# Attention and gated feed-forward in one kernel: the gain moves from the weights to the rows, the sinks get their own maximum and exp, and the reordering of q and k gets a fixed place

## The chip, the cores and the metric

One core of a Trainium2 chip runs the whole program. The metric is the device time in microseconds of one execution, lower is better. Times of several executions are given as a median with the lowest and highest. A profile is one execution recorded by the hardware profiler. The engines are PE (matmuls; PEld is its weight load), DVE (vector), ACT (activations), POOL (GpSimd) and SP, which here only issues stores. Each engine works through a queue of its own in order.

## The reference

Sliding-window attention with four sink positions for 4 batches, 8 heads, 768 positions and head size 64, followed by an RMS norm and a gated feed-forward layer over the 3072 tokens with 512 channels and 1536 hidden units.

```python
scores = scale * np.matmul(q, k.transpose(0, 1, 3, 2))
keep = is_sink | in_window          # pos < 4, or 0 <= i - j < 128
scores = np.where(keep, scores, -1e9)
a = np.exp(scores - np.max(scores, axis=-1, keepdims=True))
a = a / (np.sum(a, axis=-1, keepdims=True) + 1e-09)
x = np.matmul(a, v)                 # heads side by side: 3072 x 512
xn = x / np.sqrt(np.mean(x * x, axis=-1, keepdims=True) + 1e-06) * rms_g
g = xn @ w_gate
out = (g * (1.0 / (1.0 + np.exp(-g))) * (xn @ w_val)) @ w_out
```

## The kernel before

**Units.** The attention is cut into 48 half tiles, numbered n: a tile of 128 positions of one batch (24 tiles, six to a batch), and in it half 0 (heads 0 to 3) or half 1 (heads 4 to 7). `a_unit(n)` multiplies q and k of four heads into PSUM, for 128 keys of the tile before and 128 of its own (L269; L264 in the first tile of a batch, which has only its own keys). DVE then folds the older half into the newer with a mask (L281; L275 in the first tile), because each pair of query and column has exactly one of the two inside the window. The four sink scores, computed once a batch by `sink_unit`, are copied in front of the 128 folded scores (L285), the maximum over 132 columns is taken (L288), and ACT takes four exps (L293). POOL copies the four sink probabilities of each head into a small tile PK (L299). `b_unit` transposes the four heads and PK on PE (L308, L312), ACT copies the result out (L317), and POOL splits it with two triangular selections into the newer part cur (L325) and the older part old (L329). `c_unit` multiplies by v (L341, L348, L353), divides by the sum (L362, L363), and after half 1 takes the sum of squares (L370), of which POOL makes the reciprocal root rr (L372, L376). `d_unit` scales the row by rr (L384), transposes it (L389) and copies it into XNT (L392).

**Feed-forward.** Eight groups of three tiles. `f_unit` makes one of twelve blocks of hidden units: gate matmuls pg and value matmuls pl (L407), tanh on ACT (L412), two multiplications on DVE (L414, L418). The sigmoid is written with tanh, so the value weights carry a factor of one half. `o_unit` multiplies by the output weights (L424), ACT copies (L429), SP stores.

**The gain.** `fold_w` multiplies both weight matrices by the RMS gain, in quarters, four row blocks each: 32 instructions on DVE (L133, L137) in all.

**q and k.** `load_qk` brings half a batch with GpSimd transfers (L97), `order_unit` reorders it on DVE (q scaled, L190; k copied, L194), `qk_unit` transposes it on PE (L204) and copies it to QT (ACT, L210) and KT (DVE L214 for the lower, ACT L218 for the upper partitions), two heads at a time. `sink_unit` ends with a copy (L237) and, for the first 128 queries with sinks, a mask on POOL (L240).

**Order.** The prologue issues on POOL, in this order: q and k of batch 0 (four transfers), v of three tiles, then the weights in quarters (two transfers each, L126) with v of the other three tiles behind the first quarter, and wo (L174). Then batch 0 is reordered, transposed and its sinks made, half by half. After that there are slots, one for each n: slot n holds `a_unit(n)`, `c_unit(n-2)`, `b_unit(n-1)` and, for even n, `d_unit`. The work for batch b is put into slots relative to its first one (base = 12 b): loads of q and k at base-11, of v at base-10 to base-5, reordering at base-7 and base-5, transposes at base-6 to base-3, sinks at base-2 and base-1. The first nine slots run alone; from the tenth on six slots at a time are woven with the blocks of one feed-forward group. The program's text is only a priority: a planner places each instruction into its engine's queue when its own model says that the inputs are there, so that an instruction of a later slot can stand ahead of one of an earlier slot.

Of the kernel before, what the change touches and what calls it, by code (L numbers as in the profile page):

```python
# [16 lines left out]
P = 128  # L17
# [4 lines left out]
def kernel(  # L22
# [64 lines left out]
    PK = [const.tile([P, P], BF16, name=f"PK{i}") for i in range(3)]  # L87
# [32 lines left out]
    rmsg = const.tile([P, KTN], FP32, name="rmsg")  # L120
    nc.sync.dma_start(out=rmsg, in_=moe_rms_g.rearrange("(kt p) -> p kt", p=P))
# [8 lines left out]
    def fold_w(c):  # L130
        cols = slice(c * CW, (c + 1) * CW)
        for kt in range(KTN):
            nc.vector.tensor_scalar(  # L133
                out=wg_bf[:, kt, cols], in0=wg_bf[:, kt, cols],
                scalar1=rmsg[:, kt:kt + 1], scalar2=None, op0=ALU.mult,
            )
            nc.vector.tensor_scalar(  # L137
                out=wv_bf[:, kt, cols], in0=wv_bf[:, kt, cols],
                scalar1=rmsg[:, kt:kt + 1], scalar2=0.5, op0=ALU.mult, op1=ALU.mult,
            )  # L140

# [5 lines left out]
    for i in range(3):  # L147
        nc.gpsimd.memset(PK[i], 0.0)
# [25 lines left out]
    nc.gpsimd.dma_start(out=wo_bf, in_=moe_w_out.rearrange("(ft p) d -> p ft d", p=P))  # L174
# [3 lines left out]
    PS = {}  # L178
# [5 lines left out]
    def order_unit(b, half):  # L184

        for nm in ("q", "k"):
            so = stage.tile([P, NT, 4, D], BF16, name=f"{nm}so", tag="so", bufs=4)
            src = ST.pop((nm, b, half)).rearrange("p h (j d) -> p j h d", j=NT)
            if nm == "q":
                nc.vector.tensor_scalar(  # L190
                    out=so, in0=src, scalar1=scale, scalar2=None, op0=ALU.mult,
                )
            else:
                nc.vector.tensor_copy(out=so, in_=src)  # L194
            SO[(nm, b, half)] = so
# [27 lines left out]
    def sink_unit(b, half):  # L223

        par = b % 2
        ps = psum.tile([P, 512], FP32, name="psk", tag="b1")
        for t in range(1, NT):
            for hi in range(2):
                hp = 2 * half + hi
                c0 = (t * 2 + hi) * 2 * NS  # L230
                nc.tensor.matmul(
                    out=ps[:, c0:c0 + 2 * NS].rearrange("p (h s) -> p h s", s=NS),
                    lhsT=QT[par][:, hp, t * P:(t + 1) * P], rhs=KT[par][:, hp, :, 0:NS],
                    start=True, stop=True,
                )
        sk = spool.tile([P, NT, 4, NS], FP32, name="sk", tag="sk", bufs=4)
        nc.vector.tensor_copy(  # L237
            out=sk[:, 1:NT], in_=ps[:, 4 * NS:NT * 4 * NS].rearrange("p (t h s) -> p t h s", s=NS, h=4),
        )
        nc.gpsimd.affine_select(  # L240
            out=sk[:, 1], in_=sk[:, 1], compare_op=ALU.is_ge, fill=NEG,
            base=0, pattern=[[0, 4], [-1, NS]], channel_multiplier=1,
        )
        SINK[(b, half)] = sk
# [9 lines left out]
    def a_unit(n):  # L254
# [19 lines left out]
        if t == 0:  # L274
            nc.vector.copy_predicated(  # L275
                out=sc[:, :, P:2 * P], mask=m_first.unsqueeze(1).to_broadcast((P, 4, P)),
                data=negbig.unsqueeze(2).to_broadcast((P, 4, P)),
            )
            c0 = P
# [8 lines left out]
        nc.vector.tensor_reduce(  # L288
            out=nmax, in_=sc[:, :, c0:2 * P], axis=AX.X, op=ALU.max, negate=True,
        )  # L290
        ps = spool.tile([P, 4, NS + P], BF16, name="ps", tag="ps", bufs=3)
        for h in range(4):
            nc.scalar.activation(  # L293
                out=ps[:, h, c0 - W0:], in_=sc[:, h, c0:2 * P], func=ACT.Exp,
                bias=nmax[:, h:h + 1], scale=1.0,
            )
        PS[n] = ps
        if t > 0:
            nc.gpsimd.tensor_copy(  # L299
                out=PK[n % 3].rearrange("p (h c) -> p h c", c=32)[:, :, 0:NS], in_=ps[:, :, 0:NS],  # L300
            )

    def b_unit(n):
        t = (n // 2) % NT
        ps = PS.pop(n)
        pp = psum.tile([P, 512], FP32, name="pp", tag="b1").bitcast(BF16)
        for h in range(4):
            nc.tensor.transpose(  # L308
                out=pp[:, h * P:(h + 1) * P], in_=ps[:, h, NS:NS + P], identity=ident,
            )  # L310
        if t > 0:
            nc.tensor.transpose(  # L312
                out=pp[:, 4 * P:5 * P], in_=PK[n % 3], identity=ident,
            )
        w = 5 * P if t > 0 else 4 * P
        pt = ppool.tile([P, 5 * P], BF16, name="pt", tag="pt")
        nc.scalar.copy(out=pt[:, 0:w], in_=pp[:, 0:w])  # L317
        if t == 0:
# [5 lines left out]
        pv4 = pt[:, 0:4 * P].rearrange("p (h c) -> p h c", h=4)  # L324
        nc.gpsimd.affine_select(  # L325
            out=cur, in_=pv4, compare_op=ALU.is_ge, fill=0.0,
# [3 lines left out]
            out=old, in_=pv4, compare_op=ALU.is_gt, fill=0.0,  # L330
            base=0, pattern=[[0, 4], [-1, P]], channel_multiplier=1,
        )
        PT[n] = (pt, cur.rearrange("p h c -> p (h c)"), old.rearrange("p h c -> p (h c)"))

    def c_unit(n):
# [4 lines left out]
        if t > 0:  # L340
            nc.tensor.matmul(  # L341
                out=pv[:, 0:4 * VW], lhsT=pt[:, 4 * P:5 * P], rhs=VS[b % 2][:, half, :],
                start=True, stop=False, skip_group_check=True,
            )
        for hh in range(4):
# [33 lines left out]
    def d_unit(bt):  # L379
        g, tb = divmod(bt, GROUP)  # L380
        if tb == 0:
            XNT[g] = xtpool.tile([P, KTN, GN], BF16, name="xnt", tag="xnt")
        xr = xpool.tile([P, DM], BF16, name="xr", tag="xr")
        nc.vector.tensor_scalar(  # L384
            out=xr, in0=X16.pop(bt), scalar1=RR.pop(bt)[:, 0:1], scalar2=None, op0=ALU.mult,
# [35 lines left out]
    def o_unit(g, tb):  # L421
# [7 lines left out]
        nc.scalar.copy(out=osb, in_=po[:, 0:DM])  # L429
# [103 lines left out]
```

## Time and profile before

| | us |
|---|---|
| median of 3 runs (lowest, highest) | 342.35 (342.06, 342.65) |
| profiled execution, its own time | 341.6 |
| its span, first to last instruction | 339.9 |
| busy: PE | 278.8 (82%) |
| busy: DVE | 237.1 (70%) |
| busy: ACT | 193.9 (57%) |
| busy: POOL | 127.8 (38%) |
| scaling of the weights, L133 and L137, 32 instructions | 5.4 + 5.2 |
| copy of the sink scores, L285, 40 instructions | 6.9 |
| copy into PK, L299, 40 instructions | 8.1 |
| mean granted clock of PE | 0.925 |

Busy time is the time in which an engine had at least one instruction running; the chain of waits is followed back from the last instruction to what released it at each step. A time line has the start, the duration, the engine, the line, the operation, out and in, and in brackets the idle time before it and what ended it.

### The profile page before, as it was taken

To read this page: it belongs to the slowest core of one execution; us is meant where nothing else is said; L and a number is where in the kernel's file an instruction comes from. 1 tells how busy PE (TensorE), PEld (TensorE's weight loads), DVE (VectorE), ACT (ScalarE), POOL (GpSimd) and SP (SyncE) were. 2 spreads that over 40 slices of the span, in tenths; PEclk is the share of its full clock that TensorE was granted. 3 is DMA by queue.
4 is the path that set the end of the run, shared out by engine and by line. 5 is a ranking of instruction groups with operands and counts; after the bars stand their busy time and mean duration, and the time that the engine had idled before them with its cause. 6 is when DMAs were issued, how large, how long until landed. Compare 5 with 4: busy or idle time off the path is not lost.

```text
span 339.9 us, 5990 instructions
## 1 busy us (share of the span) xinstructions
PE 278.8 (82%) x2129; PEld 166.3 (49%) x2144; DVE 237.1 (70%) x550; ACT 193.9 (57%) x465; POOL 127.8 (38%) x257
## 2 busy tenths in 40 slices
PE   0451257598998889999988999999889999998994
PEld 0430024365654556556645556655446545554651
DVE  7687274678865897589857883898569837872850
ACT  1371145777566677776666677766566666554321
POOL 8972268889421331322413313214021423122000
PEclk9955555789999999999999999999999999999999
DMA  7999999999801000200010001000100010001002
GB/s 106 188 189 204 206 176 64 172 136 183 54 31 64 0 3 2 92 0 4 23 71 1 2 0 64 31 3 3 62 31 2 0 64 32 3 22 72 0 2 93
DMA packets 43197, 20.83 MB, mean 61 GB/s; under 512 B 26272, under 2 KB 40096, under 8 KB 43168
## 3 DMA queue, kind: packets, MB, share of 16 engines
q0 software_dynamic: 39184, 14.16, 36.5%
q1 hardware_dynamic: 3984, 6.30, 4.9%
q8 instruction: 17, 0.28, 0.3%
q14 instruction: 12, 0.10, 0.1%
HBM read 28.31 MB, written 6.29 MB: 102 GB/s over the span
## 4 chain that ended last, share of the span: by engine, by line
PE 40%; ACT 16%; DVE 14%; POOL 14%; issue 8%; DMA 8%; ACTq 0%; POOLq 0%; DVEq 0%
PE po L424 12%; PE pg L407 10%; PE pl L407 9%; ACT ps L293 7%; DMA qst<-in_q_dram 5%; DVE hT L418 4%; POOL v L106 3%; DVE p L414 3%; DVE nmax L288 3%; DMA v<-in_v_dram 2%; ACT pt L317 2%; PE s L269 2%; ACT th L412 2%; POOL rr L376 2%; POOL cur L325 2%
## 5 line engine op out<-in xcount | busy, mean ns | idle before, releaser
L407 PE MATMUL pg<-xnt,wg_bf 128*128 128x384 bf16 x384 | 79.1, 326 | 4.6 <-DVE hT L418 2.7
L407 PE MATMUL pl<-xnt,wv_bf 128*128 128x384 bf16 x384 | 78.0, 326 | 2.4 <-DVE p L414 1.2
L412 ACT ACTIVATE th<-pg 128x384 bf16<-128x384 f32 x96 | 47.6, 498 | 47.8 <-PE pg L407 46.0
L293 ACT ACTIVATE ps<-s,nmax 128x132 bf16<-128x132 f32 (+1 forms) x192 | 55.5, 372 | 33.9 <-DVE nmax L288 28.8
L424 PE MATMUL po<-wo_bf,hT 128*128 128x512 bf16 x273 | 65.1, 379 | 1.7 <-DVE hT L418 0.9
L414 DVE SCALAR_TENSOR_TENSOR p<-th,pg 128x384 bf16<-128x384 bf16 x96 | 52.5, 548 | 16.5 <-ACT th L412 15.5
L418 DVE TENSOR_TENSOR hT<-p,pl 128x384 bf16<-128x384 bf16 x96 | 52.6, 549 | 3.1
L407 PEld LDWEIGHTS <-wv_bf 128*128 128x128 bf16 x384 | 37.5, 98 | 29.6 <-issue 5.1
L407 PEld LDWEIGHTS <-wg_bf 128*128 128x128 bf16 x384 | 35.3, 98 | 25.5 <-issue 7.4
L299 POOL COPY PK<-ps 128x16 bf16<-128x16 bf16 x40 | 8.1, 203 | 97.7 <-ACT ps L293 97.6
L424 PEld LDWEIGHTS <-hT 128*128 128x128 bf16 x288 | 27.2, 98 | 30.6 <-DVE hT L418 0.9
L325 POOL TENSOR_SCALAR_AFFINE_SELECT cur<-pt 128x512 bf16<-128x512 bf16 x40 | 26.0, 651 | 41.2 <-ACT pt L317 40.2
L317 ACT COPY pt<-pp 128x640 bf16<-128x640 bf16 (+1 forms) x48 | 33.0, 687 | 12.7 <-PE pp L312 9.5
L281 DVE COPY_PREDICATED s<-m_old,s 128x512 f32<-128x512 int16 x40 | 27.7, 691 | 17.8 <-PE s L269 17.6
L308 PE MATMUL pp<-ident,ps 128*128 128x128 bf16 x192 | 24.7, 232 | 16.7 <-ACT ps L293 16.5
L288 DVE TENSOR_REDUCE nmax<-s 128x4 f32<-128x528 f32 (+1 forms) x48 | 33.5, 698 | 0.5
L269 PE MATMUL s<-KT,QT 128*128 128x512 bf16 x80 | 27.6, 420 | 4.5 <-ACT ps L293 4.5
L308 PEld LDWEIGHTS <-ps 128*128 128x128 bf16 x192 | 15.6, 102 | 26.1 <-ACT ps L293 19.0
L329 POOL TENSOR_SCALAR_AFFINE_SELECT old<-pt 128x512 bf16<-128x512 bf16 x40 | 26.9, 674 | 0.0
L384 DVE TENSOR_SCALAR xr<-x,rr 128x512 bf16<-128x512 bf16 x24 | 10.4, 432 | 20.1 <-POOL rr L376 20.1
L429 ACT COPY osb<-po 128x512 f32<-128x512 f32 x24 | 14.2, 590 | 18.0 <-PE po L424 18.0
L106 POOL DMA_DIRECT2D v<-in_v_dram x24 | 21.4, 903 | 0.9 <-issue 0.7
(64 smaller groups left out, 365.4 us busy)
## 6 DMA issues: line engine op xcount, KB each, us to landing
out_dram<-osb SPq DMA_DIRECT2D x24, 256.0 KB, 2.0
qst<-in_q_dram POOLq DMA_DIRECT2D x8, 384.0 KB, 6.5
kst<-in_k_dram POOLq DMA_DIRECT2D x8, 384.0 KB, 7.0
v<-in_v_dram POOLq DMA_DIRECT2D x24, 128.0 KB, 5.8
wg_bf<-in_moe_w_gate_dram POOLq DMA_DIRECT2D x4, 384.0 KB, 9.7
wv_bf<-in_moe_w_val_dram POOLq DMA_DIRECT2D x4, 384.0 KB, 10.9
wo_bf<-in_moe_w_out_dram POOLq DMA_DIRECT2D x1, 1536.0 KB, 19.6
rmsg<-in_moe_rms_g_dram SPq DMA_DIRECT2D x1, 2.0 KB, 2.2
```

What stands on the lines that cost most here:

```text
L106: nc.gpsimd.dma_start(out=v16[:, :, 0:D], in_=v[b, :, t * P:(t + 1) * P, :].rearrange("h t d -> t h d"),)
L269: nc.tensor.matmul(out=dst, lhsT=lhsT, rhs=KT[par][:, hp, :, (t - 1) * P:(t + 1) * P], start=True, stop=True,)
L288: nc.vector.tensor_reduce(out=nmax, in_=sc[:, :, c0:2 * P], axis=AX.X, op=ALU.max, negate=True,)
L293: nc.scalar.activation(out=ps[:, h, c0 - W0:], in_=sc[:, h, c0:2 * P], func=ACT.Exp, bias=nmax[:, h:h + 1], scale=1.0,)
L308: nc.tensor.transpose(out=pp[:, h * P:(h + 1) * P], in_=ps[:, h, NS:NS + P], identity=ident,)
L317: nc.scalar.copy(out=pt[:, 0:w], in_=pp[:, 0:w])
L325: nc.gpsimd.affine_select(out=cur, in_=pv4, compare_op=ALU.is_ge, fill=0.0, base=0, pattern=[[0, 4], [1, P]], channel_multiplier=-1,)
L407: nc.tensor.matmul(out=dst[:, 0:GN], lhsT=w[:, kt, ft * P:(ft + 1) * P], rhs=xnt[:, kt, :], start=(kt == 0), stop=(kt == KTN - 1),)
L412: nc.scalar.activation(out=th, in_=pg[:, 0:GN], func=ACT.Tanh, scale=0.5)
L414: nc.vector.scalar_tensor_tensor(out=p1, in0=th, scalar=1.0, in1=pg[:, 0:GN], op0=ALU.add, op1=ALU.mult,)
L418: nc.vector.tensor_tensor(out=h_t, in0=p1, in1=pl[:, 0:GN], op=ALU.mult)
L424: nc.tensor.matmul(out=po[:, 0:DM], lhsT=HT[(g, ft)][:, tb * P:(tb + 1) * P], rhs=wo_bf[:, ft, :], start=(ft == 0), stop=(ft == FTN - 1),)
```

## The change

**The gain.** `fold_w` is gone, and the weights stay as loaded. The gain is loaded once as a row that is repeated on all 128 partitions (grow, 32 bits). `d_unit` multiplies the row of x by rr and by grow in one DVE instruction with two tensor inputs. The factor one half moves to the last copy on ACT.

**The softmax.** `sink_unit` also takes the negated maximum of the sink scores for each query and head (sm), on DVE, behind the mask on POOL. `a_unit` no longer copies the sink scores into PSUM: it takes the maximum over 128 columns, then the smaller of the two negated maxima (DVE, 128 x 4), POOL adds it to the sink scores (sd, 128 x 16), and ACT takes four exps of 128 columns and a fifth, of the 16 sink values, which it writes straight into the place to be transposed. One tile PS of five blocks takes the place of ps and PK; the POOL copy L299 is gone.

**The reordering.** Each of the two DVE instructions of `order_unit` is pinned by `keep_in_program_order`, which ties an instruction to the one traced just before it on its engine: it can't be queued ahead of that one. The loads of q and k of batch 1 move into the prologue, ahead of wo; those of the later batches go to base-11 and base-10. The reordering goes to base-4 and base-3, the transposes of both head pairs of a half to base-3 and base-2, the sinks to base-2 and base-1.

```diff
+    grow = const.tile([P, DM], FP32, name="grow")
+    nc.sync.dma_start(
+        out=grow, in_=moe_rms_g.rearrange("(o d) -> o d", o=1).to_broadcast((P, DM)),
+    )
...
+    load_qk(1, 0)
+    load_qk(1, 1)
     nc.gpsimd.dma_start(out=wo_bf, in_=moe_w_out.rearrange("(ft p) d -> p ft d", p=P))
...
-                nc.vector.tensor_copy(out=so, in_=src)
+                ins = nc.vector.tensor_copy(out=so, in_=src)
+
+            tc.keep_in_program_order(ins)
...
-        SINK[(b, half)] = sk
+        sm = spool.tile([P, NT, 4], FP32, name="sm", tag="sm", bufs=4)
+        nc.vector.tensor_reduce(
+            out=sm[:, 1:NT], in_=sk[:, 1:NT], axis=AX.X, op=ALU.max, negate=True,
+        )
+        SINK[(b, half)] = (sk, sm)
...
-            nc.vector.tensor_copy(out=sc[:, :, W0:P], in_=SINK[(b, half)][:, t])
-            c0 = W0
         nmax = small.tile([P, 4], FP32, name="nmax", tag="nmax")
         nc.vector.tensor_reduce(
-            out=nmax, in_=sc[:, :, c0:2 * P], axis=AX.X, op=ALU.max, negate=True,
-        )
-        ps = spool.tile([P, 4, NS + P], BF16, name="ps", tag="ps", bufs=3)
+            out=nmax, in_=sc[:, :, P:2 * P], axis=AX.X, op=ALU.max, negate=True,
+        )
+        ps = PS[n % 3]
+        if t > 0:
+            sk, sm = SINK[(b, half)]
+            nc.vector.tensor_tensor(out=nmax, in0=nmax, in1=sm[:, t], op=ALU.min)
+            sd = small.tile([P, 4, NS], FP32, name="sd", tag="sd")
+            nc.gpsimd.tensor_tensor(
+                out=sd, in0=sk[:, t], in1=nmax.unsqueeze(2).to_broadcast((P, 4, NS)), op=ALU.add,
+            )
         for h in range(4):
             nc.scalar.activation(
-                out=ps[:, h, c0 - W0:], in_=sc[:, h, c0:2 * P], func=ACT.Exp,
-                bias=nmax[:, h:h + 1], scale=1.0,
-            )
-        PS[n] = ps
+                out=ps[:, h, :], in_=sc[:, h, P:2 * P], func=ACT.Exp, bias=nmax[:, h:h + 1], scale=1.0,
+            )
         if t > 0:
-            nc.gpsimd.tensor_copy(
-                out=PK[n % 3].rearrange("p (h c) -> p h c", c=32)[:, :, 0:NS], in_=ps[:, :, 0:NS],
+            nc.scalar.activation(
+                out=ps[:, 4, :].rearrange("p (h c) -> p h c", c=32)[:, :, 0:NS], in_=sd, func=ACT.Exp,
             )
...
-        nc.vector.tensor_scalar(
-            out=xr, in0=X16.pop(bt), scalar1=RR.pop(bt)[:, 0:1], scalar2=None, op0=ALU.mult,
+        nc.vector.scalar_tensor_tensor(
+            out=xr, in0=X16.pop(bt), scalar=RR.pop(bt)[:, 0:1], in1=grow, op0=ALU.mult, op1=ALU.mult,
         )
...
-        if g == 0 and ft % FPC == 0:
-            fold_w(ft // FPC)
...
-        nc.scalar.copy(out=osb, in_=po[:, 0:DM])
+        nc.scalar.activation(out=osb, in_=po[:, 0:DM], func=ACT.Copy, scale=0.5)
...
-        for half in range(2):
-            slots[base - 11].append((0.0, lambda b=b, half=half: load_qk(b, half)))
+        if b > 1:
+            for half in range(2):
+                slots[base - 11 + half].append((0.0, lambda b=b, half=half: load_qk(b, half)))
         for half in range(2):
-            slots[base - 7 + 2 * half].append((0.0, lambda b=b, half=half: order_unit(b, half)))
-        for hp in range(HP):
-            slots[base - 6 + hp].append((0.7, lambda b=b, hp=hp: qk_unit(b, hp)))
-        slots[base - 2].append((0.3, lambda b=b: sink_unit(b, 0)))
-        slots[base - 1].append((0.3, lambda b=b: sink_unit(b, 1)))
+            slots[base - 4 + half].append((0.0, lambda b=b, half=half: order_unit(b, half)))
+            for hp in (2 * half, 2 * half + 1):
+                slots[base - 3 + half].append((0.7, lambda b=b, hp=hp: qk_unit(b, hp)))
+            slots[base - 2 + half].append((0.3, lambda b=b, half=half: sink_unit(b, half)))
```

More of the change, by code (lines that the diff above doesn't have):

```diff
@@ L86 @@
     KT = [const.tile([P, HP, 2, S], BF16, name=f"KT{i}") for i in range(2)]
-    PK = [const.tile([P, P], BF16, name=f"PK{i}") for i in range(3)]
+    PS = [const.tile([P, 5, P], BF16, name=f"PS{i}") for i in range(3)]
     VS = [const.tile([P, 2, 4 * VW], BF16, name=f"VS{i}") for i in range(2)]
@@ L119 @@
     wo_bf = const.tile([P, FTN, DM], BF16, name="wo_bf")
-    rmsg = const.tile([P, KTN], FP32, name="rmsg")
-    nc.sync.dma_start(out=rmsg, in_=moe_rms_g.rearrange("(kt p) -> p kt", p=P))
+    grow = const.tile([P, DM], FP32, name="grow")
+    nc.sync.dma_start(
+        out=grow, in_=moe_rms_g.rearrange("(o d) -> o d", o=1).to_broadcast((P, DM)),
+    )
     def load_w(c):
@@ L128, in load_w @@
             )
-    def fold_w(c):
-        cols = slice(c * CW, (c + 1) * CW)
-        for kt in range(KTN):
-            nc.vector.tensor_scalar(
-                out=wg_bf[:, kt, cols], in0=wg_bf[:, kt, cols],
-                scalar1=rmsg[:, kt:kt + 1], scalar2=None, op0=ALU.mult,
-            )
-            nc.vector.tensor_scalar(
-                out=wv_bf[:, kt, cols], in0=wv_bf[:, kt, cols],
-                scalar1=rmsg[:, kt:kt + 1], scalar2=0.5, op0=ALU.mult, op1=ALU.mult,
-            )
     for i in range(2):
@@ L147 @@
     for i in range(3):
-        nc.gpsimd.memset(PK[i], 0.0)
+        nc.gpsimd.memset(PS[i][:, 4, :], 0.0)
     negbig = const.tile([P, 1], FP32, name="negbig")
@@ L177 @@
     PT = {}
-    PS = {}
     PV = {}
@@ L189, in order_unit @@
             if nm == "q":
-                nc.vector.tensor_scalar(
+                ins = nc.vector.tensor_scalar(
                     out=so, in0=src, scalar1=scale, scalar2=None, op0=ALU.mult,
@@ L278, in a_unit @@
             )
-            c0 = P
         else:
@@ L304, in b_unit @@
         t = (n // 2) % NT
-        ps = PS.pop(n)
+        w = 5 if t > 0 else 4
         pp = psum.tile([P, 512], FP32, name="pp", tag="b1").bitcast(BF16)
-        for h in range(4):
+        for h in range(w):
             nc.tensor.transpose(
-                out=pp[:, h * P:(h + 1) * P], in_=ps[:, h, NS:NS + P], identity=ident,
+                out=pp[:, h * P:(h + 1) * P], in_=PS[n % 3][:, h, :], identity=ident,
             )
[L311 to L317, printed above, removed]
+        pt = ppool.tile([P, 5, P], BF16, name="pt", tag="pt")
+        nc.scalar.copy(out=pt[:, 0:w, :].rearrange("p h c -> p (h c)"), in_=pp[:, 0:w * P])
         if t == 0:
@@ L323, in b_unit @@
         old = ppool.tile([P, 4, P], BF16, name="old", tag="old")
-        pv4 = pt[:, 0:4 * P].rearrange("p (h c) -> p h c", h=4)
         nc.gpsimd.affine_select(
-            out=cur, in_=pv4, compare_op=ALU.is_ge, fill=0.0,
+            out=cur, in_=pt[:, 0:4, :], compare_op=ALU.is_ge, fill=0.0,
             base=0, pattern=[[0, 4], [1, P]], channel_multiplier=-1,
@@ L329, in b_unit @@
         nc.gpsimd.affine_select(
-            out=old, in_=pv4, compare_op=ALU.is_gt, fill=0.0,
+            out=old, in_=pt[:, 0:4, :], compare_op=ALU.is_gt, fill=0.0,
             base=0, pattern=[[0, 4], [-1, P]], channel_multiplier=1,
         )
-        PT[n] = (pt, cur.rearrange("p h c -> p (h c)"), old.rearrange("p h c -> p (h c)"))
+        PT[n] = (pt, cur, old)
     def c_unit(n):
@@ L341, in c_unit @@
             nc.tensor.matmul(
-                out=pv[:, 0:4 * VW], lhsT=pt[:, 4 * P:5 * P], rhs=VS[b % 2][:, half, :],
+                out=pv[:, 0:4 * VW], lhsT=pt[:, 4, :], rhs=VS[b % 2][:, half, :],
                 start=True, stop=False, skip_group_check=True,
@@ L348, in c_unit @@
             nc.tensor.matmul(
-                out=dst, lhsT=cur[:, hh * P:(hh + 1) * P], rhs=V16[(b, t)][:, h, :],
+                out=dst, lhsT=cur[:, hh, :], rhs=V16[(b, t)][:, h, :],
                 start=(t == 0), stop=(t == 0), skip_group_check=True,
@@ L353, in c_unit @@
                 nc.tensor.matmul(
-                    out=dst, lhsT=old[:, hh * P:(hh + 1) * P], rhs=V16[(b, t - 1)][:, h, :],
+                    out=dst, lhsT=old[:, hh, :], rhs=V16[(b, t - 1)][:, h, :],
                     start=False, stop=True, skip_group_check=True,
@@ L383, in d_unit @@
         xr = xpool.tile([P, DM], BF16, name="xr", tag="xr")
-        nc.vector.tensor_scalar(
-            out=xr, in0=X16.pop(bt), scalar1=RR.pop(bt)[:, 0:1], scalar2=None, op0=ALU.mult,
+        nc.vector.scalar_tensor_tensor(
+            out=xr, in0=X16.pop(bt), scalar=RR.pop(bt)[:, 0:1], in1=grow, op0=ALU.mult, op1=ALU.mult,
         )
```

## The prediction

> **What bounds the kernel now.** I read the slices of the page first, then the windows, then the time lines of the queues in the first 80 us.
>
> ```profile
> PE   0451257598998889999988999999889999998994
> PEclk9955555789999999999999999999999999999999
> DMA  7999999999801000200010001000100010001002
> 78.00:304.00 226.00, 211.38 (x1667) 126.20 (x1680) 171.06 (x388) 146.93 (x367) 70.45 (x157) 1.00 0.14 30
> 70.69 1.07 PE L407 MATMUL pg<-xnt,wg_bf 128*128 128x384 bf16 x4
> ```
>
> A slice is 8.5 us. There are two stages. From 78 us on the tensor engine is full: 211.4 of 226 us in the window line (its order is PE, PEld, DVE, ACT, POOL), against 171.1 of DVE and 146.9 of ACT. Before that it is mostly idle at a granted clock near 0.5, while the transfers run at nine tenths and more. The border is the first feed-forward matmul at 70.69 us (T0 below); 269 of the 339.9 us follow it. So two questions decide: when does T0 come, and what is added behind it?
>
> What holds T0 is in the two queues that work in order, POOL and DVE:
>
> ```profile
> 18.09 0.22 DVE L237 COPY sk<-psk 128x80 f32<-128x80 f32 x1
> 20.20 0.74 POOL L126 DMA_DIRECT2D wv_bf<-in_moe_w_val_dram  x1 [0.31 <-DMA v<-in_v_dram]
> 21.27 1.87 POOL L174 DMA_DIRECT2D wo_bf<-in_moe_w_out_dram  x1 [0.34 <-DMA v<-in_v_dram]
> 23.15 0.41 POOL L240 TENSOR_SCALAR_AFFINE_SELECT sk<-sk 128x16 f32<-128x16 f32 x2
> 27.56 0.74 POOL L97 DMA_DIRECT2D kst<-in_k_dram  x1 [0.53 <-DMA wg_bf<-in_moe_w_gate_dram]
> 33.25 0.32 DVE L137 TENSOR_SCALAR wv_bf<-wv_bf,rmsg 128x384 bf16<-128x384 bf16 x1 [1.62 <-DMA wv_bf<-in_moe_w_val_dram]
> 35.07 0.71 DVE L288 TENSOR_REDUCE nmax<-s 128x4 f32<-128x528 f32 x1
> 42.79 0.56 DVE L190 TENSOR_SCALAR qso<-qst 128x1536 bf16<-128x1536 bf16 x1 [3.98 <-DMA qst<-in_q_dram]
> ```
>
> To see here: the scaling of the weights stands in DVE's queue ahead of the attention and waits for weights until 33.25 us, so the maximum of half tile n=2 starts only at 35.07; the reordering of batch 1 then waits until 42.79 for its transfer and n=3 is late again. Also: the sink scores of half 0 were copied at 18.09, but their mask (L240) ran on POOL at 23.15, behind all the transfers issued before it in the program. And a transfer's issue waits for an older one. The 17th, 18th, 19th and 23rd issue waited for the landing of the 9th, 10th, 11th and 15th: eight are outstanding, and the ninth blocks POOL. The maxima (L288) start at 19.9, 23.6, 35.1, 43.5, 49.6, 53.6, 60.2, 65.8 and 72.0 us for n=0 to 8.
>
> **What is taken away.** The 32 scalings (10.6 us of DVE) and their waits go, and so do the two stalls just shown. Were that all, n=2 would follow n=1 in about 4.1 us (the quickest step, 49.55 to 53.61) and T0 would come some 12 us sooner (11.5 and 8.4 us for n=2 and n=3 become 4.1 each).
>
> **What replaces it in the head.** The reordering is now kept behind the DVE instruction traced just before it. For half 1 of batch 0 that is the new sink maximum of half 0, which needs L240, which stands on POOL behind every transfer of the prologue, and these now include the four loads of batch 1 ahead of wo. Step by step:
> - wo is now the 23rd transfer; it waits for the 15th, which landed at 27.3 (16.30 plus 11.0). Issue 27.6 to 29.4 (1.87), L240 to 29.7.
> - Sink maximum 0.24 (priced as L237, also 80 elements), two reorderings at 0.56 (median of L190), transposes of k 0.85, two KT copies at 0.95 (L214), the upper copy 0.79 (L218): 34.6. Then for n=1 matmul 0.4, mask 0.75, maximum 0.69, exps 1.15, and for n=2 matmul 1.0 and mask 0.69: the maximum of n=2 starts near 39.8, against 35.07. The weights no longer wait for DVE, but DVE now waits for POOL.
> - POOL's queue is filled with transfers of later slots wherever the planner saw it free: all 26 loads that slots 2 to 31 issue stand between n=2 and n=10, two to five to a slot, and four loads of slot 1 between VS and n=2. From L240 to n=2's new addition (sd) there are now some 11 us with 1.3 us of other POOL work, so I take 8 or more loads there at 0.75 to 0.9 each. The eighth of these is the 31st transfer and waits for the 23rd, wo. wo lands after the 18th (33.2), four loads of q and k at 1.95 (they landed at 42.8, 44.7, 46.7, 48.6) and its own 7.7 (33.2 to 40.9): 48.7. So sd of n=2 comes near 50, and with it the exp behind it on ACT; queued behind that on ACT are the exps of n=3, on them PE's matmul of n=4.
> - From 50: 0.2, exps 1.15, matmul 1.0, mask 0.69, steps between: maximum of n=4 at 53.3 (was 49.6). From there no q/k work is left in the head: 4.1 to 4.7 a step, I take 4.4, so n=7 at 66.5. Before, T0 came 4.9 us after n=7, with 0.96 of q/k transposes ahead of it; now 4.0: T0 at 70.5.
>
> Head: 0.0 us. Its ends: 7 loads or fewer ahead of sd leave n=2 at 39.8, T0 = 39.8 + 5 x 4.4 + 4.0 = 65.8, -4.9; eleven loads, at one landing (1.0) each, +3. The grown load of g (a row for each partition, 256 KB on SP, where 2 KB took 2.2 us) can hold the first q by about 1 us; DVE is at its memsets until 7.8 anyway, and half 1 waits later still, so nothing.
>
> **What moves behind T0.** Of the four q/k units of batch 1 three ran before T0; all four now stand in slots 9 and 10. Each is 12 transposes, 0.67 us on the chain of waits: 3 x 0.67 = +2.0 us on a full PE. Their copies (DVE 0.95, ACT 1.6 a unit) find room: DVE is busy 28.1 of the 36.7 us of that group. Later batches only shift theirs inside the full stage: 0.
>
> **What is added to each tile behind T0** (33 of 40 tiles that have sinks).
>
> ```profile
> L384 DVE TENSOR_SCALAR xr<-x,rr 128x512 bf16<-128x512 bf16 x20 | 8.6, 431 | 18.4 <-POOL rr L376 18.4
> L293 ACT ACTIVATE ps<-s,nmax 128x132 bf16<-128x132 f32 x131 | 38.0, 373 | 14.5 <-DVE nmax L288 11.1 <-PE pv L348 2.0 <-POOL old L329 1.4
> L370 ACT ACTIVATION_READ_ACCUMULATOR sq<-x 128x1 f32 x19 | 4.1, 215 | 0.0
> L363 DVE TENSOR_TENSOR x<-pv,rden 128x256 bf16<-128x256 f32 x38 | 15.9, 418 | 0.2
> ```
>
> - ACT: one exp of 16 elements. No row has it; below, the step of the four exps less their elements (0.26 - 0.10 = 0.16), above, a whole exp (0.37). I take 0.21, the short ACT row: 33 x 0.21 = 6.9 us.
> - DVE: xr gets a second input of 32 bits. From 256 elements (418) to 384 (548) the two-input rows grow by 1.02 ns an element, so 512 take 0.68, against 0.35 undisturbed (median): 20 x 0.33 = +6.6. Six sink maxima +1.4. The minimum takes the place of the copy L285 (0.17; between 0.06, a memset of one column, and 0.18, L362): 0. The shorter maximum -0.4. Sum +7.6.
> - POOL: addition for copy, 0.2 for 0.2, but ACT waits for it. It has the four exps (1.15) as cover: cur and old together are 1.3, so a small part shows only where they stand right ahead.
> - PE: the same transposes; osb and masks as before: 0.
>
> How much reaches the end? In 78 to 304 the chain of waits has 20 of the 45 us of exps (45%) and some 40 of DVE's 171 (23%; hT 5.7, p 4.9, nmax 3.7 and the mask 2.6% of the window, with smaller ones): 3.1 + 1.7. PE's own queue, 94% full, is a second branch that hides part of any delay; I take half, +2.5, between -1 (the POOL copy behind the exps no longer delays the last transpose) and +5.
>
> By the Trainium skill ("ScalarE: Activation LUTs", What ACT_TABLE_LOAD costs) an ACTIVATE with immediate scale and bias takes 186 ns plus 0.833 an element, and neighbours overlap by 93 ns: an estimate of 0.11 for this exp, with which the last sum would be some 0.8 us less; the Trainium skill's 280 plus 0.833 for a pointer bias gives 387 for 128 elements and the trace has 369, so it fits. The Trainium skill ("GPSIMD Engine Reference", Key points) also says that GpSimd shares its SBUF interfaces with VectorE for instructions with two SBUF inputs, which the new xr has; the old xr already ranges from 336 to 819 ns here, so the trace agrees that this operation is stretched, and no run yet shows whether the new form is more so.
>
> **Sum:** 341.6 (the profiled execution's own time: span 339.9 and 1.7 around it) + 0.0 + 2.0 + 2.5 = 346.1. The median of the runs is 0.75 above that execution, so 346.5 for the median, rounded.
>
> **Rivals.**
> 1. *POOL is not blocked* (fewer than eight loads ahead of sd). For it: the count rests on how the planner spreads loads, not on a row. Then the head gives 4.9: 341.6 - 4.9 + 4.5 = 341.2, on the median's scale 342, about no change.
> 2. *The kept place doesn't bind*, half 1 of batch 0 is reordered near 10.6 us as before. Then n=2 waits only for L240 (29.5): T0 between 55.5 (29.5 + 22 + 4.0) and 65 (blocked by wo at n=4 or 5); middle -10, so 336.8. Against it: the program has the maximum ahead of the reordering, and L240 demonstrably stood behind the loads. This is the faster side.
> 3. *Worse:* ACT's new dependence on POOL and DVE's on L240 also cost in the full stage. POOL stands up to 3.5 us waiting for ACT's pt there; it decides from the point where sd or L240 is queued behind such a wait. Six sink maxima at 1 us and eleven loads in the head: 346.5 + 3 + 3 = 352.
>
> **Chances.** Forecast 0.45, rival 1 0.22, rival 2 0.17, rival 3 0.16. This measurement tells about 0.2% (0.7 us) from no change. Faster: 0.16 of rival 2, half of rival 1, 0.06 of the forecast's low end: 0.33. Same 0.09. Slower 0.58. The forecast's own range is 343 to 350; cases of both signs count, so the range goes from within rival 2 to rival 3: 333 to 353.
>
> **What would show it.** L240 behind wo near 29.5; the reordering of half 1 right behind the sink maximum; a load on POOL that waits for wo until about 49, with sd of n=2 behind it; T0 near 70.5; the short exp near 0.2; xr near 0.68. The prediction is wrong if half 1 is reordered before 20 us, if T0 is before 66, or if PE in the full stage stays at its 93.5%.

## The result and the profile after

The changed kernel takes 360.6 us (median of 4 runs, 360.21 to 361.25) against 342.5 for the kernel before (4 runs, 342.06 to 342.68): 1.053 times as long, 95% interval 1.0512 to 1.0553. The forecast was 346.5, with a range up to 353. The direction was right, the size was not. The profiled execution took 361.25 us, with a span of 359.4.

T0, the first feed-forward matmul, is again the border. Slices of the page of the changed kernel (9.0 us each), the time line of PE at T0, and a window of the full stage (length; then busy us of PE, PEld, DVE, ACT, POOL; granted clock; DMA share; GB/s):

```profile
PE   0304205469988899999898999998989999998995
DMA  8999999916060200010002000100010001002002
```
```profile
82.86 0.52 PE L398 MATMUL pg<-xnt,wg_bf 128*128 128x384 bf16 x1
```
```profile
90.00:316.00 226.00, 210.94 (x1668) 124.48 (x1667) 178.43 (x390) 152.30 (x395) 65.21 (x147) 0.99 0.08 26
```

T0 moved from 70.7 to 82.9 us: +12.2 in the head. From T0 to the end of the span it was 269.2 us and is 276.5: +7.3. Together that is the 19.5 us between the two spans. In PE's row no slice passes 4 tenths up to 54 us, and the DMA row stays full up to 72 us. The share of PE in the full stage (210.94 of 226, 93.3%) is nearly what it was, so that share alone doesn't show the 7 us: what was added behind T0 counts in part as busy PE.

The time line of DVE in the head of the changed kernel (start, duration, engine, line, operation, out and in; in brackets the idle time before it and what ended it; some rows are left out, and the last one is the maximum of n=4):

```profile
16.13 0.69 DVE L282 TENSOR_REDUCE nmax<-s 128x4 f32<-128x512 f32 x1
28.92 0.24 DVE L238 TENSOR_REDUCE sm<-sk 128x20 f32<-128x80 f32 x1 [12.10 <-POOL sk L233]
29.07 0.55 DVE L181 TENSOR_SCALAR qso<-qst 128x1536 bf16<-128x1536 bf16 x1
35.67 0.69 DVE L282 TENSOR_REDUCE nmax<-s 128x4 f32<-128x512 f32 x1
51.89 0.24 DVE L238 TENSOR_REDUCE sm<-sk 128x20 f32<-128x80 f32 x1 [15.53 <-POOL sk L233]
52.38 0.69 DVE L277 COPY_PREDICATED s<-m_old,s 128x512 f32<-128x512 int16 x1
53.09 0.69 DVE L282 TENSOR_REDUCE nmax<-s 128x4 f32<-128x512 f32 x1
53.82 0.16 DVE L288 TENSOR_TENSOR nmax<-nmax,sm 128x4 f32<-128x4 f32 x1
63.63 0.69 DVE L282 TENSOR_REDUCE nmax<-s 128x4 f32<-128x512 f32 x1
```

DVE does nothing for 12.1 and again for 15.5 us. Both times it stands for POOL's mask of the sink scores (L233). After the first wait comes the reordering of half 1, right behind the sink maximum; after the second the mask and maximum of n=2, at 53.09 us where it was 35.07. What POOL did meanwhile:

```profile
27.62 1.02 POOL L166 DMA_DIRECT2D wo_bf<-in_moe_w_out_dram  x1 [1.20 <-DMA wg_bf<-in_moe_w_gate_dram]
28.64 0.24 POOL L233 TENSOR_SCALAR_AFFINE_SELECT sk<-sk 128x16 f32<-128x16 f32 x1
28.83 1.84 POOL L246 COPY VS<-v 4x130 bf16<-4x130 bf16 x4
39.26 0.87 POOL L106 DMA_DIRECT2D v<-in_v_dram  x1 [1.07 <-DMA qst<-in_q_dram]
49.61 1.28 POOL L246 COPY VS<-v 4x130 bf16<-4x130 bf16 x4 [9.48 <-DMA v<-in_v_dram]
51.65 0.21 POOL L233 TENSOR_SCALAR_AFFINE_SELECT sk<-sk 128x16 f32<-128x16 f32 x1
54.93 0.25 POOL L290 TENSOR_TENSOR sd<-sk,nmax 128x16 f32<-128x16 f32 x1
```

The first mask stands behind wo. The second stands behind the copies of VS for batch 1 (slot 13 of the program, queued here by the planner), which wait 9.48 us for v of batch 1; those loads were issued behind wo, and the first of them landed at 49.6 us, behind wo at 48.5. And sd of n=2, which lets ACT finish its exps, comes at 54.93.

The new rows of the costliest groups (count, then busy us, mean ns, idle before them):

```profile
L377 DVE SCALAR_TENSOR_TENSOR xr<-x,rr,grow 128x512 bf16<-128x512 bf16 x24 | 20.5, 856 | 13.9 <-POOL rr L369 13.9
L298 ACT ACTIVATE PS<-sd 128x16 bf16<-128x16 f32 x40 | 9.2, 231 | 0.1
L290 POOL TENSOR_TENSOR sd<-sk,nmax 128x16 f32<-128x16 f32 x40 | 8.6, 216 | 55.4 <-DVE nmax L288 47.0 <-DVE rden L355 7.8
```

The fifth exp takes 0.23 us, sd 0.22, and xr a median of 0.75 us (0.35 before).

### The profile page after: what moved, and what is told of

Its sections match the earlier page's. It is cut to its first block, busy times and chain, and to the rows that moved or that the text cites. A ratio compares the mean times of both kernels' runs of the same rounds, so it can differ in the third digit from the quotient of the medians.

```text
span 359.4 us, 5954 instructions
## 1 busy us (share of the span) xinstructions
PE 282.1 (78%) x2144; PEld 165.2 (46%) x2144; DVE 239.7 (67%) x526; ACT 199.2 (55%) x505; POOL 129.0 (36%) x257
## 4 chain that ended last, share of the span: by engine, by line
PE 30%; DVE 22%; ACT 16%; POOL 13%; issue 9%; DMA 8%; POOLq 0%; ACTq 0%; DVEq 0%
PE po L415 11%; PE pg L398 7%; ACT PS L294 6%; PE pl L398 6%; DVE hT L409 5%; DMA v<-in_v_dram 5%; DVE p L405 5%; POOL v L106 3%; DMA wv_bf<-in_moe_w_val_dram 3%; ACT th L403 3%; DVE xr L377 2%; DVE s L277 2%; DVE nmax L282 2%; ACT pt L311 2%; ACT sq L363 2%
## 5 line engine op out<-in xcount | busy, mean ns | idle before, releaser
L294 ACT ACTIVATE PS<-s,nmax 128x128 bf16<-128x128 f32 x192 | 55.0, 369 | 60.4 <-DVE nmax L288 41.2
L415 PE MATMUL po<-wo_bf,hT 128*128 128x512 bf16 x288 | 67.4, 379 | 0.0
L403 ACT ACTIVATE th<-pg 128x384 bf16<-128x384 f32 x96 | 47.0, 495 | 35.1 <-PE pg L398 33.0
L318 POOL TENSOR_SCALAR_AFFINE_SELECT cur<-pt 128x512 bf16<-128x512 bf16 x40 | 26.4, 659 | 70.2 <-ACT pt L311 70.1
L307 PE MATMUL pp<-ident,PS 128*128 128x128 bf16 x232 | 25.7, 231 | 18.6 <-ACT PS L294 18.1
L282 DVE TENSOR_REDUCE nmax<-s 128x4 f32<-128x512 f32 x48 | 33.0, 687 | 0.8
L307 PEld LDWEIGHTS <-PS 128*128 128x128 bf16 x232 | 17.7, 103 | 27.8 <-ACT PS L294 19.6
L377 DVE SCALAR_TENSOR_TENSOR xr<-x,rr,grow 128x512 bf16<-128x512 bf16 x24 | 20.5, 856 | 13.9 <-POOL rr L369 13.9
L197 PE MATMUL pqk<-ident,qso 128*128 128x128 bf16 x96 | 9.3, 242 | 24.6 <-DVE qso L181 24.2
L290 POOL TENSOR_TENSOR sd<-sk,nmax 128x16 f32<-128x16 f32 x40 | 8.6, 216 | 55.4 <-DVE nmax L288 47.0
L322 POOL TENSOR_SCALAR_AFFINE_SELECT old<-pt 128x512 bf16<-128x512 bf16 x40 | 28.1, 702 | 0.0
L203 ACT COPY QT<-pqk 128x768 bf16<-128x768 bf16 x16 | 12.8, 802 | 26.1 <-PE pqk L197 26.1
```

What stands on the lines that cost most here:

```text
L282: nc.vector.tensor_reduce(out=nmax, in_=sc[:, :, P:2 * P], axis=AX.X, op=ALU.max, negate=True,)
L294: nc.scalar.activation(out=ps[:, h, :], in_=sc[:, h, P:2 * P], func=ACT.Exp, bias=nmax[:, h:h + 1], scale=1.0,)
L307: nc.tensor.transpose(out=pp[:, h * P:(h + 1) * P], in_=PS[n % 3][:, h, :], identity=ident,)
L322: nc.gpsimd.affine_select(out=old, in_=pt[:, 0:4, :], compare_op=ALU.is_gt, fill=0.0, base=0, pattern=[[0, 4], [-1, P]], channel_multiplier=1,
L403: nc.scalar.activation(out=th, in_=pg[:, 0:GN], func=ACT.Tanh, scale=0.5)
L415: nc.tensor.matmul(out=po[:, 0:DM], lhsT=HT[(g, ft)][:, tb * P:(tb + 1) * P], rhs=wo_bf[:, ft, :], start=(ft == 0), stop=(ft == FTN - 1),)
```

## The experiments

Two questions: which wait holds the head, and what costs the time behind T0. The verdicts rest on T0, on the start of the maxima, and on the time from T0 to the end of the span, which is called "behind" below. T0 and "behind" are read from one profiled execution of each version, the times are medians; the executions of one version lie 0.5 to 3.0 us apart, so a difference below 1 us in "behind" is not told from noise. Line numbers of an experiment differ by a few from those of the changed kernel.

**1. Lifting the kept place of batch 0 alone** (nopin0):

```diff
-            tc.keep_in_program_order(ins)
+            if b > 0:
+                tc.keep_in_program_order(ins)
```

> The changed kernel with the reordering of batch 0 left free (the later batches stay pinned). Theory: in the changed kernel half 1 of batch 0 waits for the sink mask, which stands on POOL behind all the loads, and the gap that this opens is filled on POOL with work that waits for wo or for what lands behind it. Without the pin half 1 is reordered before 14 us, the maxima of n=2 and n=3 start near 29.5 and 34, POOL meets the copies VS of batch 1 only behind n=3 and stands there until their v lands (49.6), so n=5 is near 54 and the first feed-forward matmul near 64 instead of 82.9. Behind it the time is as in the changed kernel (276.5): span 341, time 342 to 343. Rival: the added work of each tile and POOL's waits cost the 18 us whatever the order of batch 0: first feed-forward matmul behind 78, time 355 or more.

Measured: 347.4 us (1.014 times the kernel before, interval 1.0115 to 1.0166; the profile is of the fastest of four executions, 345.8), T0 71.2, behind 273.0. So this one kept place accounts for 13.2 of the 18.1 us. T0 didn't come at the expected 64: n=2 starts at 27.0 us now, but n=5 only at 55.9, since POOL still stands:

```profile
39.73 0.92 POOL L106 DMA_DIRECT2D v<-in_v_dram  x1 [0.80 <-DMA qst<-in_q_dram]
50.10 1.28 POOL L247 COPY VS<-v 4x130 bf16<-4x130 bf16 x4 [9.45 <-DMA v<-in_v_dram]
```

**2. The VS copies held in their place instead** (vskeep): the copies of VS of batches 1 to 3 can't come ahead of their slot; the kept place of batch 0 stays.

```diff
-            nc.gpsimd.tensor_copy(
+            ins = nc.gpsimd.tensor_copy(
                 out=VS[b % 2][32 * hh
...
+            if b > 0:
+                tc.keep_in_program_order(ins)
```

> The changed kernel with the copies VS of batches 1 to 3 on POOL kept in their place in the program, so that they can't stand in the gap ahead of n=2. Theory (any load in that gap ends up waiting for wo, because eight transfers are outstanding): the mask of half 1 moves from 51.7 to about 42, but the 31st transfer then waits for the landing of wo near 49 and four more behind it for one landing of v each, so the addition sd of n=2 stays near 54, the first feed-forward matmul within 2 us of 82.9, time 359 to 362. Rival (only the wait of these copies for the v of batch 1 blocked POOL): sd of n=2 near 43, first feed-forward matmul near 72, time about 350.

Measured: 361.2 us (one run), T0 83.4, behind 276.1. The mask of half 1 now runs at 42.43, n=2 starts at 42.8 and n=4 at 50.6, but n=5 at 63.6. The stall went one place on, to the next load:

```profile
42.43 0.21 POOL L233 TENSOR_SCALAR_AFFINE_SELECT sk<-sk 128x16 f32<-128x16 f32 x1
49.23 0.76 POOL L97 DMA_DIRECT2D kst<-in_k_dram  x1 [6.58 <-DMA wo_bf<-in_moe_w_out_dram]
54.24 0.22 POOL L292 TENSOR_TENSOR sd<-sk,nmax 128x16 f32<-128x16 f32 x1
```

That is the wait that the prediction had reckoned with (a load that waits for wo until about 49). Taking away the first thing that waits for wo gains nothing while another stands behind it.

**3. Two parts of the change alone** (no_order: gain and softmax of the change, with the order of the kernel before; gain_only: the kernel before with the gain on the rows and nothing else). Of no_order's edit, in part:

```diff
-    load_qk(1, 0)
-    load_qk(1, 1)
...
-            slots[base - 4 + half].append((0.0, lambda b=b, half=half: order_unit(b, half)))
+            slots[base - 7 + 2 * half].append((0.0, lambda b=b, half=half: order_unit(b, half)))
```

> The changed kernel with the whole reordering part undone: no pin, q and k of batch 1 loaded behind wo, the slots as before. What is left is the unscaled weights and the new softmax. Theory: half 1 is early, n=2 starts near 29.5, but the free reordering of batch 1 again stands ahead of n=3 and waits for q (42.8), so the first feed-forward matmul comes near 70.7 as before; behind it the new work of each tile costs 3 to 5: time 344 to 347. Rival (the new softmax is what costs): time 355 or more.

> The kernel before with the first part alone: weights unscaled, g on the rows of x. Theory: the weights' waits leave DVE, n=2 starts near 29.5 instead of 35.1, but the reordering of batch 1 still makes n=3 wait until 43.3, so the first feed-forward matmul stays near 70.7; behind it xr costs 0.75 instead of 0.35 us, 20 times, of which a quarter to a half reaches the end: time 343 to 346. Rival (the scaling of the weights held the head): first feed-forward matmul near 63, time 335 to 337.

Measured: no_order 349.5 us (ratio 1.0213, interval 1.0176 to 1.0249), T0 70.2, behind 276.3. gain_only 354.2 us (ratio 1.0347, interval 1.0325 to 1.0369), T0 76.2, behind 276.2. Both missed: no_order was expected at 344 to 347, gain_only at 343 to 346. Taking the scaling of the weights out of DVE's queue brought n=2 forward (29.0 us in gain_only, 35.1 before) but not T0; DVE reaches the reordering of batch 1 sooner and stands there longer, until q has landed behind wo. In gain_only:

```profile
43.68 0.56 DVE L180 TENSOR_SCALAR qso<-qst 128x1536 bf16<-128x1536 bf16 x1 [10.94 <-DMA qst<-in_q_dram]
```

and in no_order the same at 42.95 (10.57 us). n=3 in gain_only starts at 44.4 us, against 43.5 before; T0 comes even 5.5 us later than before, since xr of the third tile starts only at 72.5 us (65.5 before). So of the two stalls behind the prediction's 12 us, the second did not hang on the scaling.

Behind T0 both are some 7 us above the 269.2 of the kernel before, though no q or k unit has moved there. The granted clock fell to a half for 3.4 us twice in gain_only and once in no_order (last section); the rest was not taken apart. It is more than gain and softmax cost together in the order of experiment 6 (2.3 us).

**4. wo late, with and without the kept place** (wo_late, nopin_wo_late). If it is wo that everything waits for, it should go behind v of batch 1:

```diff
-    nc.gpsimd.dma_start(out=wo_bf, in_=moe_w_out.rearrange("(ft p) d -> p ft d", p=P))
...
+    slots[8].append((0.0, lambda: nc.gpsimd.dma_start(
+        out=wo_bf, in_=moe_w_out.rearrange("(ft p) d -> p ft d", p=P))))
```

> The changed kernel with wo issued in slot 8 of the program, behind the loads of v of batch 1; all kept places stay. Theory (the head waits for wo: whatever load POOL reaches after the prologue can only be issued or used behind wo's landing near 49 us): v of batch 1 now lands near 42 us, so the mask of sink half 1 runs near 40, the maximum of n=2 starts at 41 to 45 us (53.1 in the changed kernel), T0 comes at 70 to 75 us (82.9), and the time is 348 to 353 us. Rival (the kept place alone costs it, wo is not what POOL stands for): the maximum of n=2 stays above 50 us, T0 at 80 or later, 358 us or more.

> The changed kernel without the kept place of batch 0's reordering, and with wo issued in slot 8. Theory (the two stalls are separate and both are gone here): the maximum of n=5, which came at 55.9 us with the kept place alone lifted, starts at 46 to 49 us, T0 comes at 61 to 65 us, what follows T0 stays 273 us, and the time is 336 to 340 us. Rival (the head is bound by the transfers themselves, 10 MB that no order of issues makes shorter): n=5 at 54 or later, T0 at 69 or later, 345 us or more.

Measured: wo_late 351.1 us (two runs; ratio 1.0263, interval 1.0237 to 1.0288), T0 74.5, n=2 at 41.1. nopin_wo_late 333.1 us (ratio 0.9736, interval 0.9721 to 0.975), T0 58.2, n=5 at 42.7, behind 272.8. With wo late POOL waits 1.5 us for v where it waited 9.48. In wo_late:

```profile
39.67 1.01 POOL L438 DMA_DIRECT2D wo_bf<-in_moe_w_out_dram  x1 [1.01 <-DMA qst<-in_q_dram]
40.73 0.21 POOL L232 TENSOR_SCALAR_AFFINE_SELECT sk<-sk 128x16 f32<-128x16 f32 x1
42.44 1.28 POOL L245 COPY VS<-v 4x130 bf16<-4x130 bf16 x4 [1.50 <-DMA v<-in_v_dram]
```

Time and T0 (us) of the four versions:

| | wo in the prologue | wo in slot 8 |
|---|---|---|
| kept place of batch 0 | 360.6, T0 82.9 | 351.1, T0 74.5 |
| none | 347.4, T0 71.2 | 333.1, T0 58.2 |

Each of the two edits works alone, and together they gain 27.5 us, some 5 more than the sum of the two (13.2 + 9.5): with the kept place in, half 1 stays late, with early wo, POOL stays blocked. All four move the same bytes; the order of issues and queues sets T0.

**5. The kept place kept, with less ahead of it** (pins_ahead): in the program both halves of batch 0 are reordered and transposed before either sink unit.

```diff
         qk_unit(0, 2 * half)
         qk_unit(0, 2 * half + 1)
+    for half in range(2):
         sink_unit(0, half)
```

> The changed kernel with all its kept places, but in the program both halves' reordering and transposes of batch 0 come ahead of the two sink units. Theory (a kept place costs nothing by itself; it cost what stood ahead of it, the sink maximum behind the mask behind the loads): half 1 is reordered before 15 us, T0 comes at 71 us as with the kept place of batch 0 lifted (71.2), what follows T0 is 273 us, and the time is 345 to 349 us. Rival for the head (a kept place delays the reordering whatever stands ahead of it): T0 near 83, 358 us or more. Rival for the full stage (the 2.5 us that the kernels with the kept place lose in the first group come from the kept place as such): T0 at 71, but 275 to 276.5 us behind it, 348 to 351 us.

Measured: 346.2 us (ratio 1.0127, interval 1.011 to 1.0144), T0 71.4, behind 273.6. All the kept places are in, and the 12 us are gone; the sink maxima still come only at 29.2 us, but no reordering is behind them any more:

```profile
13.42 0.66 DVE L181 TENSOR_SCALAR qso<-qst 128x1536 bf16<-128x1536 bf16 x1
14.01 0.95 DVE L185 COPY kso<-kst 128x1536 bf16<-128x1536 bf16 x1
29.19 0.40 DVE L238 TENSOR_REDUCE sm<-sk 128x20 f32<-128x80 f32 x2 [1.79 <-POOL sk L233]
```

So it was never the kept place as such, but what the program has ahead of it.

**6. What costs behind T0: gain and softmax apart.** All four combinations were run in one head: no kept place in batch 0, the changed kernel's reordering for batches 1 to 3, wo in slot 8, q and k of batch 1 in slots 1 and 2 (the expectations say slots 5 and 6). Where the weights are scaled, the scaling is held in slots 2 to 9, an eighth to a slot.

```diff
-    load_qk(1, 0)
-    load_qk(1, 1)
...
+    for i in range(2 * NCH):
+        slots[2 + i].append((0.0, lambda i=i: fold_half(i // 2, i % 2)))
```

> The kernel before (scaled weights, old softmax) with q and k of batch 1 loaded in slots 5 and 6 of the program, wo in slot 8, the scaling of the weights held in slots 2 to 9, an eighth to a slot, and the changed kernel's later, kept reordering of batches 1 to 3. Theory (the head of both kernels is set by what stands ahead of the half tiles in the queues of DVE and POOL): no step from n=1 to n=8 is longer than 6 us, T0 comes at 56 to 64 us against 70.7, and what follows it grows by the 2 to 3 us of q/k units behind T0 (271 to 272): 328 to 337 us. Rival (transfers bind): T0 stays at 68 or later, 340 us or more.

> The changed kernel (gain on the rows, new softmax) without the kept place of batch 0, with q and k of batch 1 loaded in slots 5 and 6 and wo in slot 8. Theory: the same head as the version with the old softmax, T0 at 56 to 64 us; what follows T0 is 273 us, as with the kept place of batch 0 alone lifted: 330 to 338 us, and the difference to the version with the old softmax is the price of xr, fifth exp and sd in the full stage, 1 to 4 us. Rival (the new softmax and xr cost nothing behind T0): the two are within 1 us where their T0 are.

> The version with q and k of batch 1 loaded early and wo late (333.0 us with gain on the rows and the new softmax, 331.9 us with neither), with gain on the rows and the old softmax. If the gain on the rows (xr 0.75 instead of 0.43 us) is what costs the 2.3 us behind T0, what follows T0 is 272.5 to 273.5 us here; if the new softmax is, it is 270 to 271 us. T0 at 56 to 60 us either way, time 329 to 333 us.

> The same with scaled weights and the new softmax. If the gain on the rows is what costs the 2.3 us behind T0, what follows T0 is 270 to 271 us here; if the new softmax is (fifth exp, sd, minimum), it is 272.5 to 273.5 us; if each has a share, in between, and the two shares add up to 2.3 us. T0 at 57 to 61 us, time 330 to 334 us.

Measured (median; T0; behind):

| | weights scaled | gain on the rows |
|---|---|---|
| old softmax | 331.9; 59.6; 270.6 | 334.1; 60.0; 272.7 |
| new softmax | 328.1; 57.5; 269.0 | 333.0; 57.9; 272.9 |

The old-softmax version with scaled weights, which has none of the two, is 270.6 - 269.2 = 1.4 us longer behind T0 than the kernel before. All four q and k units of batch 1 stand behind T0 there, where the kernel before has one, but 1.4 is not shown to be their price: before_wo_late (experiment 8), which moves none of them, has 270.5. Gain and softmax together add 2.3 (272.9 - 270.6). But they don't share it: the gain on the rows costs 2.1 us with the old softmax and 3.9 with the new one, while the new softmax gains 1.6 us with scaled weights and costs 0.2, which is nothing, with the gain on the rows. In the times, head included, the gain costs 2.2 and some 5 us, and the softmax gains 3.8 and 1.1. The expectation for softmax_early_qk had 270 us as its lowest. A row and a window of it:

```profile
L386 DVE TENSOR_SCALAR xr<-x,rr 128x512 bf16<-128x512 bf16 x24 | 11.2, 468 | 12.3 <-POOL rr L378 12.3
```
```profile
65.00:291.00 226.00, 214.54 (x1704) 127.46 (x1716) 178.48 (x402) 153.89 (x403) 73.97 (x162) 1.00 0.19 35
```

and of new_softmax_early_qk, which differs only in where the gain stands:

```profile
L375 DVE SCALAR_TENSOR_TENSOR xr<-x,rr,grow 128x512 bf16<-128x512 bf16 x24 | 20.5, 853 | 12.5 <-POOL rr L367 12.5
```
```profile
65.00:291.00 226.00, 211.07 (x1681) 125.69 (x1691) 181.50 (x396) 152.28 (x395) 73.76 (x156) 1.00 0.21 35
```

In the same 226 us DVE is busy 3 us longer and PE does 3.5 us less. The fifth exp and sd are in both, and ACT's last copy osb takes 0.60 us with the factor and 0.59 without it. So it is xr, 0.75 us instead of 0.35, that costs.

**7. The gain row in 16 bits** (gain16_early_qk), from the version with both:

```diff
+    growb = const.tile([P, DM], BF16, name="growb")
+    nc.scalar.copy(out=growb, in_=grow)
...
-            out=xr, in0=X16.pop(bt), scalar=RR.pop(bt)[:, 0:1], in1=grow, op0=ALU.mult, op1=ALU.mult,
+            out=xr, in0=X16.pop(bt), scalar=RR.pop(bt)[:, 0:1], in1=growb, op0=ALU.mult, op1=ALU.mult,
```

> The version with gain on the rows and the new softmax, with the row of g held in 16 bits. If it is the 32-bit second input that stretches xr, it falls from 0.75 to 0.45 to 0.55 us, and what follows T0 loses up to 1 us; if the two-input form itself does, xr stays at 0.70 to 0.75 us and the time at 333 us.

Measured: 333.3 us (333.0 with 32 bits), behind 273.5, and xr unchanged (median 750 ns against 752):

```profile
L377 DVE SCALAR_TENSOR_TENSOR xr<-x,rr,growb 128x512 bf16<-128x512 bf16 x24 | 20.7, 862 | 11.2 <-POOL rr L369 11.2
```

It is the form with a second tensor that costs, not its 32 bits.

**8. The kernel before with wo late** (before_wo_late), the same edit as in 4:

> The kernel before with one edit: wo issued in slot 8 of the program. Theory (the kernel before, too, pays in its head for wo ahead of q, k and v of batch 1): the maximum of n=2 stays at 35 us, since the scaling of the weights still holds it, but q of batch 1 lands some 7 us sooner, n=3 starts at 36 to 40 us (43.5), T0 comes at 63 to 67 us (70.7), what follows it stays 269 us: 334 to 338 us. Rival (wo mattered only for the changed kernel's sink mask and loads on POOL): 341 to 343 us.

Measured: 339.5 us (ratio 0.9913, interval 0.9894 to 0.9931), T0 67.9, behind 270.5. It gains 3.0 us, about half of what was expected. n=2 is at 28.2 us already, not 35, since the scaling that waits for later weights no longer stands ahead of it; then DVE waits for q of batch 1 and n=3 starts at 38.1 (expected 36 to 40), but the steps up to T0 don't shorten any further:

```profile
35.82 0.56 DVE L189 TENSOR_SCALAR qso<-qst 128x1536 bf16<-128x1536 bf16 x1 [3.82 <-DMA qst<-in_q_dram]
```

**The best version** is softmax_early_qk: 328.1 us, 0.9583 times the kernel before (interval 0.9568 to 0.9598). It keeps of the change the new softmax and the later reordering with its kept places from batch 1 on, drops the gain on the rows and the kept place of batch 0, holds the scaling of the weights in slots 2 to 9, loads q and k of batch 1 in slots 1 and 2, and issues wo late.

## Why the prediction was wrong

**The head, forecast 0.0, measured +12.2.** The first half of the mechanism was the one forecast, and came out nearly to the number: wo issued at 27.62 (27.6), the sink mask of half 0 behind it, done by 28.9 (29.7), half 1 reordered right behind the sink maximum at 29.07, wo landed at 48.5 (48.7). The step that failed is "the maximum of n=2 starts near 39.8". It followed the transposes, the matmuls and the exps of half 1, but not half 1's own sink unit: a second mask on POOL, and a second sink maximum on DVE ahead of n=2. By then POOL had taken six loads and the VS copies of batch 1, which wait for v, and v lands behind wo. So n=2 was at 53.09, 13.3 us later than forecast, and the maximum of n=4 at 63.6 instead of 53.3: +10.3. The forecast had POOL blocked by wo, but by an eighth load, and let only sd of n=2 stand behind the block; the VS copies weren't in it. The three steps from n=4 to n=7 took 15.8 us (63.6 to 79.4), not 13.2: +2.6. T0 came 3.4 us after n=7, not 4.0: -0.6. Together, before rounding, 12.4, which is T0 at 82.9 instead of 70.5. vskeep shows that the forecast's own block, a load that waits for wo until 49.2 (forecast: 48.7), costs as much by itself (T0 83.4): after it come four more loads before sd, which starts at 54.24, where the forecast had it near 50. Two sums of the prediction are also off, by half a microsecond: the terms up to the maximum of n=2 add up to 39.3, not 39.8, and 346.1 with 0.75 is 346.9, not 346.5.

**What moves behind T0, forecast +2.0:** old_softmax_early_qk is 1.4 longer behind T0. That is near the forecast, but doesn't show that the three q and k units cost it, since before_wo_late is 1.3 longer without them.

**What is added to each tile, forecast +2.5 (-1 to +5):** 2.3, measured in the order of experiment 6. The sum was right, its parts were not: that they cancelled was luck. The forecast gave the larger part to ACT's fifth exp (3.1 of the chain, before the half was taken) and the smaller to DVE, xr above all (1.7). The runs show xr to cost 2.1 to 3.9, and the softmax with its fifth exp to cost at most 0.2, or to gain 1.6. The single durations were sound: exp 0.23 (0.21), sd 0.22 (0.2), xr 0.75 (0.68). What went wrong is the share of them that reaches the end. For the softmax the likely reason, which no run isolates, is what it displaces: a copy of the sink scores between mask and maximum, and a POOL copy between exps and transposes. The forecast set these off against the new instructions by their busy time (the minimum for the copy, sd for the POOL copy) and not by where they stand.

**What was not in the sum: 3.6 us** behind T0 (7.3 less 1.4 and 2.3). The stretch from the first gate matmul of a group to that of the next tells where they lie. The second group takes 34.1 us in the changed kernel and 32.7 to 32.8 in vskeep, wo_late and new_softmax_early_qk: some 1.3 us, in the group in which the granted clock falls in this profiled execution (last section). The other three executions, with a mean clock of 1.00 on record, have spans 0.3 to 0.9 us shorter. The rest, some 2.5 us, lies in the first group, and only in the kernels whose half 1 comes late: 42.3 us in the changed kernel, 42.4 in wo_late and 43.0 in vskeep, against 39.7 to 40.7 in nopin0, pins_ahead, nopin_wo_late and new_softmax_early_qk. Which instructions it is was not settled.

**The rivals.** That POOL is not blocked and that the kept place doesn't bind both fell (experiments 1, 2 and 4). Rival 3, "worse", had the right sign and named the two places, six more sink maxima and loads in the head, but put 3 us on each; the head alone cost 12.4 more than forecast. The test "PE in the full stage stays at its 93.5%" was a poor one: the share stayed at 93.3% and the stage still became 7.3 us longer.

## What to carry to other kernels

Before keeping an instruction in its program place, follow what stands ahead of it on every queue up to the load that the last one waits for; the place costs nothing by itself, and 12 us with a mask behind a large load ahead of it. A large transfer that is needed last should be issued last, since here everything issued behind it landed behind it, at 49.6 us or later; and when one wait on it is removed, look for the next before expecting a gain. An operation taken off a queue is worth what its successors can then do: the scaling of the weights was in front of a transfer that was just as late, and moving it onto the rows turned a one-input instruction into a two-input one of twice the length.

## What the runs showed of the hardware

**The second input.** At 512 elements the DVE multiplication by a number for each partition takes 0.35 us at the median, with a second tensor of 32 bits 0.75 (new_softmax_early_qk), and 0.75 again when all tensors have 16 bits (gain16_early_qk). The Trainium skill ("VectorE: DVE Perf Modes", The perf-mode tier table) gives a two-tensor operation with 16-bit operands double rate; for this three-operand form no such gain shows.

**The clock.** In the profiled execution of the changed kernel the granted clock fell to a half for 3.4 us at a group's border, where PE waits for the exps and then for the last XNT. Two windows of the same length, before and in it:

```profile
121.90:125.30 3.40, 1.81 (x20) 1.02 (x19) 1.93 (x6) 2.70 (x8) 0.21 (x1) 1.00 0.09 35
125.30:128.70 3.40, 3.40 (x12) 1.66 (x11) 1.53 (x5) 1.63 (x6) 0.21 (x1) 0.50 0.12 44
```

PE was busy 1.81 of the 3.4 us before, not idle. It happens twice in gain_only (at 112.2 and 259.0 us, behind 1.49 and 1.56 us of work), once in no_order (at 254.5 us, behind 1.56), and not in nopin_wo_late, where PE was busy 1.93 us at the same border. The amount of work alone doesn't decide it: no_order keeps its clock behind a stretch with 1.70 (104.3 to 107.7 us). The Trainium skill ("TensorE: Matmul & The Clock Gate", What's actually happening) has the gate close after an idle window of about 3.4 us that runs freely. The length agrees with the 3.4 us seen here; that the window must be idle does not, since PE worked in more than half of it here.

The record of the clock is not complete either. In vskeep it stands at 1.00 from the first to the last instruction, yet a score matmul (L268) ahead of T0 takes up to 0.63 us there, as in the changed kernel, where the record has one half, and 0.38 us behind T0. So a mean clock of 1.00 doesn't show that the head ran at full clock.
